# Chunk 3's Q, K and V as one run of paired half-height products, chunk 4's moved into the second gate-up stage, and the first down stage's pieces at given tiles

## The chip, the cores and the metric

The kernel runs on one core of one Trainium2 chip. The metric is device time in microseconds (us), the median over runs. The core's engines are TensorE (PE, matrix products; its weight loads are listed as PEld), VectorE (DVE), ScalarE (ACT), GpSimd (POOL) and SyncE (SP). Every engine works through its own instructions in the order in which the program emits them; they meet through semaphores. SP and POOL issue most transfers; these land later, moved by the core's 16 DMA engines.

## The reference

A transformer block with conditioning: a layer norm, modulated by a row vector; attention with 32 heads of 18 columns, in which each position sees 8 positions at distance 2; a residual; a second norm; a gated bilinear feed-forward (the gate has no nonlinearity); a second residual. All in bfloat16, with 2048 positions, D = 576 and F = 4608.

```python
mod = (silu(c) @ w_mod).reshape(1, 6, 1, 576)        # sa, ca, ga, sb, cb, gb
h = layernorm(x) * (1 + ca) + sa
q, k, v = split(h @ wqkv)                            # 32 heads of 18
idx = pos[:, None] - 2 * arange(8)[None, :]          # masked where negative
attn = softmax(q . k[idx] * 18 ** -0.5)
x = x + ga * ((attn . v[idx]) @ wo)
h = layernorm(x) * (1 + cb) + sb
x = x + gb * (((h @ w_gate) * (h @ w_up)) @ w_down)
```

## The kernel before

**Tiling.** Positions are cut into 8 chunks of 256 (two row tiles of 128) for the attention part, and into 5 groups of row tiles for the feed-forward (`GROUPS`, L43): tiles 0-1, 2-5, 6-9, 10-12 and 13-15. Group 1 is chunks 1 and 2. For each group there is a gate-up stage (`gate_up`, L758) and then a down stage (`down`, L814). What the attention part of later chunks needs is put as small pieces among the products of these stages: an attention piece is a Python function that emits its instructions when it is called, so the order of calls is the order of work on every engine.

**Down stage.** For each of the 36 steps `f` (128 rows of the hidden dimension each) and each row tile `j` of the group, `mm_a` multiplies by 512 columns of the down weights and `mm_r` by the remaining 64; the sums stay in PSUM banks (8 in all; the first down stage keeps 3). The last four steps run tile by tile, so that the evictions of one tile run beside the products of the next. Down weights come in blocks of four steps: when block b is done, block b + 3 is asked for on POOL's queue, into the buffer that became free (3 buffers). `spread` (L748) sets the pieces at equal distances over the steps.

**Pieces of chunk i, by name.** `a_ln`: statistics of the first norm (DVE). `a_norm`: reciprocal deviation (ACT, two instructions), normalization (DVE). `a_t`: ten transposes (PE), then five modulated column blocks into `hT`, by default three on DVE and two on ACT. `a_q` (5 groups) and `a_v` (2 row tiles): Q, K and V by plain products with 128 rows of contraction; the 576 rows are 4.5 times 128, and the fifth product's lower half is zero. `b_mul`, `b_add`: attention times values, summed (DVE); the last writes `o_sb`. `b_o`: output transposes (PE), three copies into `oT` (ACT). `b_w(i, j)`: output projection of a row tile (PE), gate and residual (DVE), giving `x1`. `b_ln`, `b_norm`: second norm. `b_t`: transposes (PE) and the modulated columns into `h2T` (three DVE, two ACT): the operand of the group's gate-up stage. In the first down stage, `gb_row` makes the feed-forward's gate row, chunk 1 and chunk 2 go through `b_o` to `b_t`, chunk 3 and chunk 4 through `a_ln` to `a_v`, and `av2` holds the fourteen value pieces of chunk 2.

**Pairs of half-height products.** A product with 64 rows of contraction uses half the array, and two of them, on the upper and the lower rows (`LO`, `HI`, L526), run side by side. `pair_unit` (L542) takes two results at once: in `first`, one is built from the upper 64 rows of the five row blocks and the other from the lower ones; in `second`, after a wait for the last product of its own `first` (`swap_after`), the halves change places. Nine half steps then do what five whole ones did, if the odd 64 rows of the contraction lie in both halves: `load_pair_rows` (L535) copies the last 64 rows of the Q, K and V weights into the lower half (SP transfers, a POOL copy into `wq4`, and two ACT copies of the modulation). `qkv_units` (L565) makes five such units of a chunk: Q, K, the fifth tile of Q and K, and two of V. In `gate_up` units stand between the steps: the `first` of the next item goes ahead of the `second` of the one before. `PAIRED` (L42) names the chunks whose Q, K and V are made like this: 5 in the second gate-up (its last steps), 6 in the third (its first steps), 7 in the fourth.

**Queues around it.** `ahead` (L803) emits the loads of later gate-up weights on SP; `gb_row` (L1157) emits POOL's loads of down weight blocks 1 and 2 and of chunk 2's values.

Of the kernel before, what the change touches and what calls it, by code (L numbers as in the profile page):

```python
# [28 lines left out]
FT = FF // P  # L29
# [6 lines left out]
FB = 4  # L36
# [2 lines left out]

MODK = (0, 4, 1, 2, 3)  # L40
QKK = (0, 1, 4, 2, 3)
PAIRED = (5, 6, 7)  # L42
GROUPS = [(0, 2), (2, 6), (6, 10), (10, 13), (13, 16)]  # L43


# [1 line left out]
def kernel(  # L47
# [133 lines left out]
    def behind(dma, load):  # L181
        tc.add_manual_dep(dma.ins, load.ins.name, SYNC, reason="value rows go first")
# [168 lines left out]
    def a_norm(i):  # L351
        aa[i]["rsq"]()
        aa[i]["norm"]()
# [181 lines left out]
    def load_pair_rows():  # L535
        nc.sync.dma_start(wqk[64:, KF, :], A_wqkv[KF * P:D, 0:2 * D])
        nc.sync.dma_start(wv[64:, KF, :], A_wqkv[KF * P:D, 2 * D:3 * D])
        nc.gpsimd.tensor_copy(halves(wq4[64:, KF, :]), halves(wqk[64:, KF, :])[:, :, KF * P:D])
        for r in (LO, HI):
            nc.scalar.copy(modc[r, 0:2, KT], modc[0:64, 0:2, KF])  # L540
# [24 lines left out]
    def qkv_units(i, plan):  # L565
        qT, kT = qTs[i % 2], kTs[i % 2]
        vs = []

        def qk_op(m, cols=slice(0, CH)):
            return lambda k: (qk_w(k, m), aa[i]["hT"][:, k, cols])  # L570

        def v_op(j, hf):
            return lambda k: (aa[i]["hT"][:, k, js(j)], wv[:, k, 288 * hf:288 * (hf + 1)])

        def q_out(a, b):
            nc.scalar.copy(qT[:, 0:2, :], a[:])
            nc.scalar.copy(qT[:, 2:4, :], b[:])

        def k_out(a, b):
            nc.scalar.copy(kT[:, 0:2, HALO:], a[:])  # L580
            nc.scalar.copy(kT[:, 2:4, HALO:], b[:])

        def qk4_out(a, b):
            for j, t in enumerate((a, b)):
                nc.scalar.copy(kT[0:64, KF, HALO + j * P:HALO + (j + 1) * P], t[64:P, 0, :])
                nc.scalar.copy(qT[:, KF, js(j)], t[:, 0, :])
            a_halo(i)

        def v_out(hf):
            def out_(a, b):  # L590
                for j, t in enumerate((a, b)):
                    if hf == 0:
                        vs.append(vstage.tile([P, DH, H], BF, name="v_sb"))
                    nc.scalar.copy(vs[j][:, :, 16 * hf:16 * (hf + 1)], t[:, 0, :].rearrange("p (h d) -> p d h", d=DH))
                    if hf == 1:
                        r0 = HALO + i * CH + j * P
                        nc.gpsimd.dma_start(vd[r0:r0 + P, :], vs[j][:].rearrange("p d h -> p (d h)"))
            return out_

        units = ([pair_unit(CH, [(qk_op(m), qk_op(m + 2)) for m in (0, 1)], q_out),  # L600
                 pair_unit(CH, [(qk_op(m), qk_op(m + 2)) for m in (KT, KT + 1)], k_out),
                 pair_unit(P, [(qk_op(KF, js(0)), qk_op(KF, js(1)))], qk4_out)]
                + [pair_unit(288, [(v_op(0, hf), v_op(1, hf))], v_out(hf)) for hf in range(2)])
        return {f: units[a:b] for f, a, b in plan}

    keyed = []

# [195 lines left out]
    def ahead(gi, n):  # L803
        g = gi * NBLK + n + 2
        if gi > 0:
            load_wgu(g)
        elif n in (1, 2, 3):
            load_wgu(g + 2)
        elif n == 4:
            load_wgu(NBLK - 1)  # L810
        elif n in (6, 7, 8):
            load_wgu(n + 3)

    def down(gi, hh, bg):  # L814
        t0, t1 = GROUPS[gi]
        nj = t1 - t0
        final = gi == NG - 1
        last = FT - (2 if final else 1) * FB
        at = spread([(1.0, p) for p in bg], last)
        acc = [ps([P, 512], F32, "acc") for _ in range(nj - final)]  # L820
        halves = [(ps([P, CH], F32, "acc"), slice(CH * h, CH * (h + 1))) for h in range(2)] if final else []
        accr = ps([P, 2 * ST, 64], F32, "accr")

        def mm_a(f, j):
            wb = wd_blk[gi * NBLK + f // FB]
            for a, cs in [(acc[j], slice(0, 512))] if j < len(acc) else halves:
                nc.tensor.matmul(a[:], lhsT=hh[:, f, js(j)], rhs=wb[:, f % FB, cs], start=(f == 0), stop=(f == FT - 1))  # L827

        def mm_r(f, j):
            wb = wd_blk[gi * NBLK + f // FB]  # L830
            nc.tensor.matmul(accr[:, j, :], lhsT=hh[:, f, js(j)], rhs=wb[:, f % FB, 512:D],  # L831
                             start=(f == 0 and j == 0), stop=(f == FT - 1), skip_group_check=True)

        for f in range(last):
            for j in range(nj):
                mm_a(f, j)
                mm_r(f, j)
            if f % FB == FB - 1:
                load_wd(gi * NBLK + f // FB + 3)
            for piece in at[f]:  # L840
                piece()
        xs = [x1[t // ST][t % ST] for t in range(t0, t1)]
        if final:
            for j in range(nj):
                for f in range(last, FT - FB):
                    mm_r(f, j)
            for j in range(len(acc)):
                for f in range(last, FT - FB):
                    mm_a(f, j)
        for j in range(nj):  # L850
            for f in range(FT - FB, FT):
                mm_r(f, j)
        o_ts = [gup.tile([P, 512], BF, name="o_t", tag="g_sb" if j % 2 else "u_sb") for j in range(nj)]
        t_r = smp.tile([P, 2 * ST, 64], BF, name="t_r", tag="tree")
        nc.vector.tensor_tensor(t_r[:, 0:nj, :], accr[:, 0:nj, :],
                                gb_bc[:, None, 512:D].to_broadcast([P, nj, 64]), ALU.mult)
        if final:
            for j in range(nj):
                nc.vector.tensor_tensor(xs[j][:, 512:D], t_r[:, j, :], xs[j][:, 512:D], ALU.add)
            for j in range(nj):  # L860
                r0 = (t0 + j) * P
                for a, cs in [(acc[j], slice(0, 512))] if j < nj - 1 else halves:
                    for f in range(FT - FB if j < len(acc) else last, FT):
                        wb = wd_blk[gi * NBLK + f // FB]
                        nc.tensor.matmul(a[:], lhsT=hh[:, f, js(j)], rhs=wb[:, f % FB, cs], start=False, stop=(f == FT - 1))
                    nc.vector.tensor_tensor(o_ts[j][:, cs], a[:], gb_bc[:, cs], ALU.mult)
                    nc.vector.tensor_tensor(xs[j][:, cs], o_ts[j][:, cs], xs[j][:, cs], ALU.add)
                    stored = slice(0, CH) if cs.stop == CH else slice(cs.start, D)
                    nc.sync.dma_start(out_flat[r0:r0 + P, stored], xs[j][:, stored])
            return  # L870
        for j in range(nj):
            for f in range(last, FT):
                mm_a(f, j)
            nc.vector.tensor_tensor(o_ts[j][:], acc[j][:], gb_bc[:, 0:512], ALU.mult)
        for j in range(nj):
            r0 = (t0 + j) * P
            nc.vector.tensor_tensor(xs[j][:, 0:512], o_ts[j][:], xs[j][:, 0:512], ALU.add)
            nc.vector.tensor_tensor(xs[j][:, 512:D], t_r[:, j, :], xs[j][:, 512:D], ALU.add)
            nc.sync.dma_start(out_flat[r0:r0 + P, :], xs[j][:])
        load_wd(gi * NBLK + NBLK + 2)  # L880
# [264 lines left out]
           3: B_one(7, [(0.0, lambda: b_ld(7, 0)), (0.0, lambda: behind(b_ld(7, 1), wgu_in[3 * NBLK + 4]))], B_av(7)) + [res(7)],  # L1145
           4: [(1.0, nop), (1.0, early_wd)]}
    av2 = [p for _, p in B_av(2)]
    oq = out_qkv(1, 3)
    first = []
    while oq or av2:  # L1150
        if oq:
            first.append(oq.pop(0))
        if len(first) > 3:
            first += [p for p in av2[:2]]
            del av2[:2]

    def gb_row():  # L1157
        mod_row(lambda p, k: wm5[p, k, :] if k < KF else wm5r[p, :], gb_bc, sc_bc2)()
        behind(load_wd(1), wgu_in[4])
        behind(b_ld(2, 0), wgu_in[7])  # L1160
        load_wd(2)
        b_ld(2, 1)

    dbg = {0: [gb_row] + first + out_qkv(2, 4) + [load_pair_rows],
           1: out_qkv(3, 5) + out_qkv(4, 6),
           2: out_qkv(5, 7) + out_qkv(6, 8),
           3: [nop, lambda: b_t(6, (1,))] + out_qkv(7, 8)}
    units = {1: qkv_units(5, [(29, 0, 1), (30, 1, 2), (31, 2, 3), (32, 3, 4), (33, 4, 5)]),
             2: qkv_units(6, [(0, 0, 1), (1, 1, 2), (2, 2, 3), (3, 3, 4), (4, 4, 5)]),
             3: qkv_units(7, [(0, 0, 3), (1, 3, 4), (2, 4, 5)])}  # L1170
    for gi in range(NG):
# [3 lines left out]
            hhp = pool("hhp", 1)  # L1175
        hh = hhp.tile([P, FT, 2 * CH], BF, name="hh") if gi else hh0
        gate_up(gi, hh, gbg.get(gi, []), units.get(gi, {}), 2 if gi == 3 else 0)
        down(gi, hh, dbg.get(gi, []))


# [28 lines left out]
```

## Time and profile before

| | us |
|---|---|
| median of 3 runs | 555.68 |
| lowest, highest | 555.51, 556.32 |
| the profiled execution | 556.14 |
| its span | 554.4 |

The granted clock was 1.00 throughout. The profile is of the one profiled execution, and its times count from the start of the span. By the order of time, the first gate-up ends and the first down stage starts with a product at 88.96; the second gate-up's first product is at 132.59, the second down stage's at about 213.4, the third gate-up's at 256.66.

A row of the page's groups gives instructions of one line, engine, tile and shape: how many, their summed busy time, and the mean duration of one. Matmuls overlap, so their durations (0.38 us for 512 columns) are longer than the distance from one start to the next (0.21 us), and PE's cost is read from starts. A row of a table by stretch has the length, then busy time and count of PE, PEld, DVE, ACT and POOL, then the granted clock, DMA share and GB/s. In an order of time each row has start, duration (of the merged run), engine, line, operation, result and operands, shapes and count, and in brackets the idle time before it with what ended it.

| first down stage, 88.96 to 132.59 | start to start, us |
|---|---|
| one step of two row tiles (0.22 + 0.03, twice) | 0.49 |
| gb row, 89.46 to 90.68 | 1.22 |
| output transposes, 91.17 to 91.73 | 0.56 |
| projection of a row tile, 96.90 to 98.12 | 1.22 |
| chunk 3's transposes, 94.86 to 96.14 (waits in it) | 1.28 |
| value product of a row tile, 109.93 to 111.15 | 1.22 |

### The profile page before, as it was taken

To read this page: it belongs to the slowest core of one execution; us is meant where nothing else is said; L and a number is where in the kernel's file an instruction comes from. 1 tells how busy PE (TensorE), PEld (TensorE's weight loads), DVE (VectorE), ACT (ScalarE), POOL (GpSimd) and SP (SyncE) were. 2 spreads that over 40 slices of the span, in tenths; PEclk is the share of its full clock that TensorE was granted. 3 is DMA by queue.
4 is the path that set the end of the run, shared out by engine and by line. 5 is a ranking of instruction groups with operands and counts; after the bars stand their busy time and mean duration, and the time that the engine had idled before them with its cause. 6 is when DMAs were issued, how large, how long until landed. Compare 5 with 4: busy or idle time off the path is not lost.

```text
span 554.4 us, 14594 instructions
## 1 busy us (share of the span) xinstructions
PE 544.1 (98%) x6160; PEld 323.9 (58%) x6195; DVE 330.5 (60%) x796; ACT 251.8 (45%) x592; POOL 63.7 (11%) x98
## 2 busy tenths in 40 slices
PE   7999999999999999999999999999999999999997
PEld 4888886665444465555544445556656555555564
DVE  7888898985669763557267786444627615322202
ACT  2746666344565664212656553113566511455500
POOL 3102201123000001112000100111100022200010
PEclk9999999999999999999999999999999999999999
DMA  8999999746646844336624775435595665976031
GB/s 267 273 286 321 348 316 329 221 145 195 228 150 195 272 147 141 97 122 196 244 80 151 238 224 176 128 100 160 189 289 173 196 189 182 319 224 186 2 86 32
DMA packets 70155, 108.38 MB, mean 195 GB/s; under 512 B 3690, under 2 KB 57850, under 8 KB 70090
## 3 DMA queue, kind: packets, MB, share of 16 engines
q1 hardware_dynamic: 58832, 61.50, 36.6%
q0 software_dynamic: 11168, 45.81, 25.9%
q8 instruction: 48, 0.79, 0.6%
q10 hardware_dynamic: 90, 0.15, 0.1%
q14 instruction: 17, 0.14, 0.1%
HBM read 103.00 MB, written 4.44 MB: 194 GB/s over the span
## 4 chain that ended last, share of the span: by engine, by line
PE 84%; DMA 9%; DVE 6%; ACT 1%; issue 1%; SPq 0%
PE pg L529 28%; PE pu L529 22%; PE acc L827 19%; PE pp L529 4%; PE accr L831 3%; DMA wgr<-in_B_w_gate_dram 3%; PE pw L674 2%; DMA wo<-in_A_wo_dram 2%; PE lg L448 2%; DMA wgu<-in_B_w_gate_dram 1%; DMA x_t<-in_A_x_dram 1%; DVE vsh L501 1%; PE pq L385 1%; DVE ln_xn L272 1%; DMA wmA<-in_w_mod_dram 1%
## 5 line engine op out<-in xcount | busy, mean ns | idle before, releaser
L529 PE MATMUL pg<-h2T,wgu 64*128 64x512 bf16 (+2 forms) x1440 | 279.1, 333 | 0.0
L529 PE MATMUL pu<-h2T,wgu 64*128 64x512 bf16 (+2 forms) x1440 | 278.3, 333 | 0.0
L529 PEld LDWEIGHTS <-wgu 64*128 64x128 bf16 x2880 | 140.4, 94 | 105.0
L785 ACT CAST u_sb<-pu 128x512 bf16<-128x512 f32 (+2 forms) x180 | 90.1, 500 | 130.6 <-PE pg L529 128.7
L827 PE MATMUL acc<-wd,hh 128*128 128x512 bf16 (+1 forms) x522 | 131.0, 372 | 0.2
L791 DVE TENSOR_TENSOR hh<-g_sb,u_sb 128x512 bf16<-128x512 bf16 (+2 forms) x180 | 66.1, 369 | 106.3 <-ACT g_sb L786 104.3
L831 PE MATMUL accr<-wd,hh 128*128 128x64 bf16 x528 | 93.7, 193 | 1.2
L786 ACT CAST g_sb<-pg 128x512 bf16<-128x512 f32 (+2 forms) x180 | 91.4, 508 | 0.0
L827 PEld LDWEIGHTS <-hh 128*128 128x128 bf16 x588 | 55.3, 98 | 59.5 <-issue 1.7
L529 PE MATMUL pg<-h2T,wgr 64*128 64x512 bf16 (+2 forms) x180 | 60.2, 334 | 0.2 <-DMA wgu<-in_B_w_gate_dram 0.2
L529 PE MATMUL pu<-h2T,wgr 64*128 64x512 bf16 (+2 forms) x180 | 60.2, 334 | 0.0
L166 POOL DMA_DIRECT2D wd<-in_B_w_down_dram x41 | 30.8, 751 | 237.1 <-PE accr L831 213.5
L831 PEld LDWEIGHTS <-hh 128*128 128x128 bf16 x576 | 51.7, 98 | 1.7
L501 DVE TENSOR_TENSOR vsh<-vsh,attn 128x1152 bf16<-128x1152 bf16 x56 | 40.4, 750 | 0.0
L438 DVE TENSOR_TENSOR prod<-qT,kT 128x1280 bf16<-128x1280 bf16 x46 | 37.1, 828 | 4.3 <-ACT kT L364 4.3
L529 PEld LDWEIGHTS <-wgr 64*128 64x128 bf16 x360 | 17.6, 94 | 16.3 <-issue 3.6
L427 POOL DMA_DIRECT2D vsh<-vd x14 | 12.5, 894 | 118.2 <-DVE o_sb L512 83.1
L676 DVE TENSOR_TENSOR x<-pw,ga_bc 128x512 bf16<-128x512 f32 x14 | 9.6, 687 | 25.7 <-PE pw L674 25.7
L294 DVE TENSOR_SCALAR h2T<-tr_pA,modc 128x256 bf16<-128x256 bf16 (+1 forms) x27 | 8.8, 382 | 26.2 <-PE tr_pA L307 26.2
L267 ACT ACTIVATE ln_rstdb<-ln_mvb,eps 128x2 f32<-128x2 f32 (+1 forms) x9 | 2.7, 296 | 44.6 <-DVE ln_mvb L264 44.6
L296 ACT ACTIVATE h2T<-tr_pB,modc 128x256 bf16<-128x256 bf16 (+1 forms) x16 | 7.7, 533 | 30.5 <-PE tr_pB L307 30.5
L508 DVE TENSOR_TENSOR vsh<-vsh 128x1152 bf16<-128x1152 bf16 x28 | 20.5, 750 | 0.0
(219 smaller groups left out, 553.4 us busy)
## 6 DMA issues: line engine op xcount, KB each, us to landing
wd<-in_B_w_down_dram POOLq DMA_DIRECT2D x41, 576.0 KB, 4.4
wgu<-in_B_w_gate_dram SPq DMA_DIRECT2D x45, 512.0 KB, 4.2
wgu<-in_B_w_up_dram SPq DMA_DIRECT2D x45, 512.0 KB, 5.7
vsh<-vd POOLq DMA_DIRECT2D x14, 1152.0 KB, 8.5
x_r<-in_A_x_dram SPq DMA_DIRECT2D x8, 288.0 KB, 7.3
vsh<-in_B_w_down_dram POOLq DMA_DIRECT2D x4, 576.0 KB, 9.4
out_dram<-x SPq DMA_DIRECT2D x15, 144.0 KB, 4.3
x_t<-in_A_x_dram SPq DMA_DIRECT2D x7, 288.0 KB, 6.7
```

The lines of the kernel that those rows point to most:

```text
L166: return nc.gpsimd.dma_start(wb[:], B_w_down[r0:r0 + FB * P, :].rearrange("(k p) n -> p k n", p=P))
L427: return nc.gpsimd.dma_start(vsh[:].rearrange("p w d h -> p w (d h)"), vsrc)
L438: nc.vector.tensor_tensor(prod[:], aa[i]["qT"][:], aa[i]["kT"][:, :, off:off + CH], ALU.mult)
L448: nc.tensor.matmul(b["lg"][H * wl:H * (wl + 1), wq, :], lhsT=ind[:, m, :], rhs=b["prod"][4 * wq + wl][:, m, :], start=(m == 0), stop=(m == ...
L501: nc.vector.tensor_tensor(v, v, at, ALU.mult)
L508: nc.vector.tensor_tensor(vsh[:, d], vsh[:, d], vsh[:, 4 + 2 * s:6 + 2 * s], ALU.add)
L529: return nc.tensor.matmul(dst, lhsT=lhs, rhs=rhs, start=first, stop=last, skip_group_check=True)
L785: nc.scalar.copy(u[:, 0:N], pu[:, 0:N])
L786: nc.scalar.copy(g[:, 0:N], pg[:, 0:N])
L791: nc.vector.tensor_tensor(hh[:, f, 0:N], g[:, 0:N], u[:, 0:N], ALU.mult)
L827: nc.tensor.matmul(a[:], lhsT=hh[:, f, js(j)], rhs=wb[:, f % FB, cs], start=(f == 0), stop=(f == FT - 1))
L831: nc.tensor.matmul(accr[:, j, :], lhsT=hh[:, f, js(j)], rhs=wb[:, f % FB, 512:D], start=(f == 0 and j == 0), stop=(f == FT - 1), skip_grou ...
```

## The change

Chunks 3 and 4 join the paired ones. Chunk 3's five units are run as one block (`qkv_block`) after step 11 of the first down stage: V's two units, the deviation of chunk 1's second norm, Q and K, then the fifth tile; inside each of the three, the `first` of all units goes before the `second` of all. Chunk 4's units go into the second gate-up's first five steps. The pieces of the first down stage are no longer spread evenly but stand at steps given by hand (several in other orders than before: the first value pieces of chunk 2 ahead of chunk 3's normalization); its two `a_t` leave one column block to DVE and four to ACT. Chunk 2's second norm is done by row tile, `b_t` of its first tile after step 31, and of its second one between the last products of the two row tiles. The pair rows are loaded during the first gate-up, and put in place within `gb_row`.

```diff
-PAIRED = (5, 6, 7)
+PAIRED = (3, 4, 5, 6, 7)
...
     def load_pair_rows():
         nc.sync.dma_start(wqk[64:, KF, :], A_wqkv[KF * P:D, 0:2 * D])
         nc.sync.dma_start(wv[64:, KF, :], A_wqkv[KF * P:D, 2 * D:3 * D])
+
+    def place_pair_rows():
         nc.gpsimd.tensor_copy(halves(wq4[64:, KF, :]), halves(wqk[64:, KF, :])[:, :, KF * P:D])
         for r in (LO, HI):
             nc.scalar.copy(modc[r, 0:2, KT], modc[0:64, 0:2, KF])
...
+    def qkv_block(i, between):
+        q, k, qk4, v0_, v1_ = qkv_units(i, [(0, 0, 5)])[0]
+        for pair in ((v0_, v1_), (q, k), (qk4,)):
+            for part in range(2):
+                for unit in pair:
+                    unit[part]()
+            if pair[0] is v0_:
+                between()
...
         elif n == 4:
             load_wgu(NBLK - 1)
+        elif n == 5:
+            load_pair_rows()
         elif n in (6, 7, 8):
             load_wgu(n + 3)
-    def down(gi, hh, bg):
+    def down(gi, hh, bg, late=nop):
...
-        at = spread([(1.0, p) for p in bg], last)
+        at = bg if gi == 0 else spread([(1.0, p) for p in bg], last)
...
         for j in range(nj):
             for f in range(last, FT):
                 mm_a(f, j)
+            if j == 0:
+                late()
             nc.vector.tensor_tensor(o_ts[j][:], acc[j][:], gb_bc[:, 0:512], ALU.mult)
...
-    oq = out_qkv(1, 3)
-    first = []
-    while oq or av2:
-        if oq:
-            first.append(oq.pop(0))
-        if len(first) > 3:
-            first += [p for p in av2[:2]]
-            del av2[:2]
-
     def gb_row():
         mod_row(lambda p, k: wm5[p, k, :] if k < KF else wm5r[p, :], gb_bc, sc_bc2)()
         behind(load_wd(1), wgu_in[4])
         behind(b_ld(2, 0), wgu_in[7])
+        place_pair_rows()
         load_wd(2)
         b_ld(2, 1)
 
-    dbg = {0: [gb_row] + first + out_qkv(2, 4) + [load_pair_rows],
+    ln2 = []
+
+    def last_ln(j):
+        if j == 0:
+            ln2.extend(ln_parts(lambda j: x1[2][j], "b"))
+            bb[2]["xn"] = ln2[0]
+        else:
+            x_res.pop(2)
+        ln2[1](j)
+        ln2[2](slice(j, j + 1))
+
+    def last_norm(j):
+        ln2[3](j)
+
+    def av(n):
+        for p in av2[:n]:
+            p()
+        del av2[:n]
+
+    at0 = [[] for _ in range(FT - FB)]
+    for f, piece in ((0, gb_row), (0, lambda: a_ln(3)), (1, lambda: b_o(1)), (2, lambda: av(2)), (3, lambda: (a_norm(3), load_x(5))),
+                     (4, lambda: b_w(1, 0)), (5, lambda: av(2)), (6, lambda: a_t(3, (0,))), (7, lambda: b_w(1, 1)), (8, lambda: av(2)),
+                     (9, lambda: b_ln(1)), (10, lambda: av(1)), (11, lambda: qkv_block(3, bb[1]["rsq"])), (11, lambda: bb[1]["norm"]()), (12, lambda: av(4)),
+                     (13, lambda: b_t(1)), (15, lambda: av(3)), (19, lambda: a_ln(4)), (22, lambda: b_o(2)), (23, lambda: (a_norm(4), load_x(6))),
+                     (25, lambda: b_w(2, 0)), (25, lambda: last_ln(0)), (26, lambda: b_w(2, 1)), (26, lambda: last_ln(1)), (27, lambda: a_t(4, (0,))),
+                     (30, lambda: last_norm(0)), (30, lambda: last_norm(1)), (31, lambda: b_t(2, (0,)))):
+        at0[f].append(piece)
+
+    dbg = {0: at0,
            1: out_qkv(3, 5) + out_qkv(4, 6),
...
-    units = {1: qkv_units(5, [(29, 0, 1), (30, 1, 2), (31, 2, 3), (32, 3, 4), (33, 4, 5)]),
+    units = {1: qkv_units(4, [(0, 0, 1), (1, 1, 2), (2, 2, 3), (3, 3, 4), (4, 4, 5)]) | qkv_units(5, [(29, 0, 1), (30, 1, 2), (31, 2, 3), (32, 3, 4), (33, 4, 5)]),
...
-        down(gi, hh, dbg.get(gi, []))
+        down(gi, hh, dbg.get(gi, []), (lambda: b_t(2, (1,))) if gi == 0 else nop)
```

## The prediction

> **What bounds the kernel now.** I read the page first: busy shares and the chain that ended last.
>
> ```profile
> PE 544.1 (98%) x6160; PEld 323.9 (58%) x6195; DVE 330.5 (60%) x796; ACT 251.8 (45%) x592; POOL 63.7 (11%) x98
> ...
> PE 84%; DMA 9%; DVE 6%; ACT 1%; issue 1%; SPq 0%
> ```
>
> TensorE (PE) sets the time over the whole, so a change is worth what it takes off PE, unless PE then waits. Next, busy time by stretch: the first down stage (88.96 to 132.59 us, from its first product to the next stage's first) and the third gate-up, which already opens with paired Q, K and V as the second one will.
>
> ```profile
> 88.96:132.59 43.63, 42.62 (x381) 26.95 (x386) 35.15 (x91) 19.76 (x52) 10.14 (x15) 1.00 0.63 193
> ...
> 256.66:336.00 79.34, 79.34 (x859) 39.15 (x860) 55.21 (x112) 44.51 (x88) 5.42 (x7) 1.00 0.60 193
> ```
>
> VectorE (DVE; behind the length come PE, weight loads, DVE) is busy 35.15 of the down stage's 43.63 us: it has not much less to do than PE. The chain of waits, in order of time, says so too:
>
> ```profile
> 106.13 2.07 DVE vsh L501 x3
> 108.20 1.10 DVE ln_xn L272 x4
> ...
> 117.45 0.61 DVE x L676
> 118.10 1.24 PE pw L674 x5
> ```
>
> Up to 118 us this stage's chain runs through DVE; only behind that, where Q, K, V of chunk 4 lie, through PE. DVE's own order of time shows that it is through early and then waits for PE:
>
> ```profile
> 123.35 1.18 DVE L272 TENSOR_SCALAR ln_xn<-x,ln_mvb,ln_rstdb 128x576 bf16<-128x576 bf16 x4 [0.60 <-ACT ln_rstdb L268]
> 127.19 1.05 DVE L294 TENSOR_SCALAR h2T<-tr_pA,modc 128x256 bf16<-128x256 bf16 x3 [2.65 <-PE tr_pA L307]
> 130.96 0.29 DVE L855 TENSOR_TENSOR t_r<-accr,gb_bc 128x128 bf16<-128x128 f32 x1 [2.73 <-PE accr L831]
> ```
>
> So PE work that leaves this stage's end is gained only until DVE's chain, ending at 124.5 us, becomes the end.
>
> **The change, part by part.** Prices are start-to-start distances on PE.
>
> ```profile
> 100.08 1.26 PE L385 MATMUL pq<-hT,wqk 128*128 128x256 bf16 x10
> 101.18 0.38 PE L827 MATMUL acc<-wd,hh 128*128 128x512 bf16 x1
> 101.39 0.19 PE L831 MATMUL accr<-wd,hh 128*128 128x64 bf16 x1
> 101.42 0.38 PE L827 MATMUL acc<-wd,hh 128*128 128x512 bf16 x1
> ```
>
> ```profile
> 260.78 2.13 PE L529 MATMUL pp<-hT,wqk 64*128 64x256 bf16 x36
> 262.75 0.38 PE L529 MATMUL pu<-h2T,wgu 64*128 64x512 bf16 x1
> ```
>
> *Q, K, V of a chunk.* Plain: ten products 1.09 us, so 4.5 such groups 4.91; V twice 1.22 (109.93 to 111.15): 7.35. Paired, in the third gate-up: 1.09 + 1.97 + 1.15 + 0.83 + 1.11 + 0.49 (each from the unit's start to the next gate-up product) = 6.64. Two chunks: 1.4 us less PE work, and one chunk's 6.64 moves into the second gate-up. There I charge it in full: the third gate-up carries the same units in the same five places and has 79.34 busy of 79.34.
>
> *What remains in the down stage.* One of its 36 steps (two row tiles) takes 0.49. I followed PE, DVE and ScalarE (ACT) piece by piece, each in its order, with rows' durations; the same count over the old order puts the next stage's first product at 132.47, where the trace has 132.59.
>
> Steps 0 to 11: 5.89 and the gb row 1.22, output transposes 0.56, projections 2 x 1.22, chunk 3's transposes 0.56, which wait 0.78 for DVE's normalization (two value products now stand before it): 88.96 to 100.4. The block: V 2.20, then 0.17 until V's first bank is evicted, Q and K 3.92, the fifth Q/K tile 0.28 + 0.22 with a wait of 0.20 between (its second half waits for its own first half, and step 12 is queued behind), and a change to 64 rows and back, 2 x 0.10 as at the stage's start (88.75 to 88.96 where a product takes 0.11): 107.6. Steps 12 to 22 with chunk 1's transposes: 113.5.
>
> The Trainium skill, TensorEngine Tiling (Array Packing), Key Properties, says that changing the tiling mode drains TensorE, which speaks against a paired block among full-height products. As an estimate from it, each change would cost the rest of a 0.27 us product, 0.16, and the stage would be 0.12 longer; the row of 0.10 decides.
>
> *The new end.* Chunk 2's output transposes end at 114.1. Behind them, one after the other: ACT's three oT copies to 115.6, the reciprocal deviation of chunk 4 (queued behind these copies) to 116.1, DVE's normalization 1.32, x of tile 4 1.22, its statistics 0.95, x of tile 5 1.22, statistics 0.95, one hT column block 0.32, normalization of tile 4 0.64: 122.7. PE has its 32 steps done at 121.5 and waits 1.28. Then transposes 0.28, 64-column remainder 0.23, four steps 0.86, transposes 0.28, four steps 0.86, switch 0.10: 125.4. ACT is later: the last deviation ends at 122.4, behind it four hT blocks (4 x 0.455) and four halves of h2T (4 x 0.345): 125.6. The second gate-up starts at 125.66, 6.81 before the 132.47 of the same count.
>
> **Sum:** -6.81 + 6.64 = -0.17 us: the 1.4 us of pairing and some 2 us of old waits come back as new waits (0.78 + 0.17 + 0.20 + 1.28 + 0.28 = 2.71). The profiled execution took 556.14 with a span of 554.4; less 0.2 it is 555.9, and the median of 555.68 becomes 555.5.
>
> *Moved at no cost.* The two transfers of the pair rows (0.22 MB) go on SP's queue from 126.8 and 130.7 us to behind weight block 8 (issued 69.5 to 72.2) and before block 9 (77.4): cover is the idle quarter of the DMA at 76 to 80 us (share 0.77 and 0.72); without it they delay by 0.6 us (0.22 MB at 350 GB/s) blocks that the second gate-up needs 30 us later. POOL's copy of 0.29 moves from 132.16 to between the issues at 79.68 and 91.11, into 10.55 us of POOL idling. ACT's two copies (0.40) move from 131.15 to 91.44, before the oT copies of 91.82; oT is then late by some 0.02, and its reader stands two steps later than before. Chunk 3's value rows leave at 104 instead of 112 us, chunk 4's some 11 us later than now, both long before they are read. Two modulations less per chunk on DVE (4 x 0.32) are four more on ACT (0.455 each): counted above.
>
> *Bounds where no row shows the thing.* Waits of PE in the new stage: none at best, 2.7 less; bank of Q: at worst it waits for V's last eviction, 0.9 more instead of 0.17 (I take the oldest bank first). Second gate-up: at best its own waits near 185 us (0.9) vanish, at worst its evictions queue (about 1). Down weights: below.
>
> **Rivals.**
> 1. *The tiles hide the waits* (faster). If statistics, normalizations and evictions fall into PE's 32 steps, PE never waits: -0.17 - 2.71, so 552.8; half of it, 554.2. For it: DVE's total shrinks by 1.3 us, and its old waits for ACT (0.60 three times) could close. Against: tile 4's and 5's x, statistics and normalization stand behind chunk 2's projection, PE's own late product.
> 2. *Down weights come late* (slower). Block 6 of the down weights is asked for when step 15 frees its buffer, 110.1, and used at step 24, 114.6: 4.5 us, since steps 14 to 22 now run bare. Landings in this stage took from 4.4 us (late in it) to 7.1. Lateness up to 0.35 hides behind DVE's normalization of chunk 4; from a landing of 4.85 on it shifts the end one for one: at 5.4, 556.0; at 7.1, 2.25 more, 557.8. For it: six of the nine landings issued from 91 to 130 us took over 4.85. Against: five of these six were issued before 108 us, with DMA shares of 0.5 to 1.0; from 112 to 122 us, with less traffic as there would be here, they took 4.4 to 4.7.
> 3. *The moved units don't fit* (slower). The second gate-up has chunk 5's units and transposes too; ACT is busy 46.5 of 80.8 us there. If evictions of chunk 4 hold banks, a wait of 0.2 at each of five units: 556.5. Against: the third gate-up.
>
> **How the numbers follow.** A measurement of this kernel tells about 0.2%, 1.1 us, from no change. Forecast 50% (its own range 554.6 to 556.4), rival 1 25%, rival 2 15%, rival 3 10%. Faster: four fifths of rival 1 and a fifth of the forecast's, 0.30. Slower: two thirds of rivals 2 and 3 and some of the forecast, 0.23. The rest, 0.47, within. Range 553.2 to 557.2: below lies only rival 1 in full, above only the latest landing.
>
> **What would show it.** After: the first gate-up product of the second group at 125.7 (123 for rival 1, over 127 for rival 2); a PE wait near 121.5 released by DVE's normalization, ACT as the last releaser; step 24's wait, if any, released by a DMA of the down weights; paired products of 2.2 + 3.9 + 0.7 us in one run; the second gate-up 87.4 long. It is wrong if DVE ends before PE's step 31, if a bank or weight wait over 0.5 us stands in the block or at step 24, or if the second gate-up grows by other than 6.6.

## The result, and the profile after

| | before | after |
|---|---|---|
| median of 22 runs, us | 555.58 | 556.76 |
| lowest, highest | 554.88, 557.02 | 555.90, 558.17 |
| the profiled execution, its span | 556.14, 554.4 | 556.8, 555.1 |
| first down stage, first product to the next stage's first | 43.63 | 38.23 |
| second gate-up, likewise | 80.85 | 87.49 |

The changed kernel takes 1.002 of the time before (95% interval 1.0014 to 1.0026): 1.2 us slower. The two stages say the same: -5.40 + 6.64 = +1.24. The second down stage has its 43.22 us in both. So the place to look is the first down stage, which was to become 6.81 us shorter.

First the changed kernel's page: busy time, share of the span and instructions of each engine; and the shares of the chain of waits.

```profile
PE 543.2 (98%) x6283; PEld 326.2 (59%) x6317; DVE 329.5 (59%) x795; ACT 254.5 (46%) x604; POOL 65.8 (12%) x98
...
PE 83%; DMA 9%; DVE 3%; issue 2%; ACT 1%; POOL 0%; SPq 0%; POOLq 0%
```

PE has 0.9 us less work, and the program is 1.2 us longer. The table by stretch (length, then PE, weight loads, DVE, ACT, POOL; granted clock, DMA share, GB/s) shows where PE stands still:

```profile
88.37:126.60 38.23, 34.81 (x376) 21.88 (x381) 34.07 (x91) 17.60 (x51) 8.95 (x13) 1.00 0.74 235
126.60:214.09 87.49, 87.44 (x999) 47.20 (x998) 58.94 (x123) 51.30 (x106) 6.38 (x9) 1.00 0.55 179
```

In the down stage 3.42 us without work on PE, where it was 1.01 before; in the second gate-up 0.05. The chunk that moved there is paid at full price, as forecast, and nothing more. PE's order of time names the places, each with the idle time and what ended it in brackets:

```profile
100.48 2.38 PE L529 MATMUL pp<-wv,hT 64*128 64x288 bf16 x36 [0.92 <-ACT hT L296]
...
107.62 0.39 PE L840 MATMUL acc<-wd,hh 128*128 128x512 bf16 x1
...
115.82 0.38 PE L840 MATMUL acc<-wd,hh 128*128 128x512 bf16 x1 [1.03 <-DMA wd<-in_B_w_down_dram]
...
123.44 0.34 PE L307 MATMUL tr_pA<-ident,ln_xn 128*128 128x128 bf16 x3 [0.53 <-DVE ln_xn L272]
...
126.60 0.37 PE L529 MATMUL pg<-h2T,wgr 64*128 64x512 bf16 x1 [0.47 <-ACT h2T L296]
```

Four waits, 2.95 us together: at the block's start for ACT's column blocks, at step 24 for down weights, for the second norm of tile 4, and for ACT's last columns. The block itself is well sized (100.48 to 107.62, 7.14; forecast 7.19). The first two waits are new; the chain of waits (start, us, what) leads through both to the late end:

```profile
98.96 1.47 ACT hT L296 x3
...
100.48 1.91 PE pp L529 x28
...
110.61 5.17 DMA wd<-in_B_w_down_dram
...
115.82 0.38 PE acc L840
...
116.96 1.09 PE pw L685 x5
...
118.08 0.18 DVE x L687
```

Two steps on, behind steps 24 and 25, comes the output projection of tile 4 (116.80 in PE's order, 116.96 in the chain), and everything of the stage's end, x, statistics, normalization, columns, is queued behind that product on DVE and ACT. A wait of PE at step 24 therefore moves the end, though PE waits for DVE anyway later.

DVE's order of time, two rows, answers to the ones shown of before:

```profile
118.08 0.69 DVE L687 TENSOR_TENSOR x<-pw,ga_bc 128x512 bf16<-128x512 f32 x1 [0.86 <-PE pw L685]
...
122.96 1.31 DVE L272 TENSOR_SCALAR ln_xn<-x,ln_mvb,ln_rstdb 128x576 bf16<-128x576 bf16 x4
```

DVE waits 0.86 for PE's late projection: in my count it had no such gap. Its last normalization is no longer preceded by a wait for ACT (0.60 before).

### The profile page after: what moved, and what is told of

The parts are those of the page before. It is cut to its first block, busy times and chain, and to the rows that moved or that the text cites. A ratio compares the mean times of both kernels' runs of the same rounds, so it can differ in the third digit from the quotient of the medians.

```text
span 555.1 us, 14848 instructions
## 1 busy us (share of the span) xinstructions
PE 543.2 (98%) x6283; PEld 326.2 (59%) x6317; DVE 329.5 (59%) x795; ACT 254.5 (46%) x604; POOL 65.8 (12%) x98
## 4 chain that ended last, share of the span: by engine, by line
PE 83%; DMA 9%; DVE 3%; issue 2%; ACT 1%; POOL 0%; SPq 0%; POOLq 0%
PE pg L529 28%; PE pu L529 22%; PE acc L840 19%; PE pp L529 5%; PE accr L844 3%; DMA wgr<-in_B_w_gate_dram 3%; PE pw L685 2%; DMA wo<-in_A_wo_dram 2%; PE lg L448 2%; DMA wgu<-in_B_w_gate_dram 1%; DMA x_t<-in_A_x_dram 1%; DMA wd<-in_B_w_down_dram 1%; DMA wmA<-in_w_mod_dram 1%; ACT hT L296 1%; PE tr_pA L307 0%
## 5 line engine op out<-in xcount | busy, mean ns | idle before, releaser
L294 DVE TENSOR_SCALAR h2T<-tr_pA,modc 128x128 bf16<-128x128 bf16 (+1 forms) x30 | 9.5, 371 | 24.7 <-PE tr_pA L307 24.7
L529 PE MATMUL pp<-hT,wqk 64*128 64x256 bf16 x360 | 22.0, 269 | 0.0
```

The lines of the kernel that those rows point to most:

```text
L529: return nc.tensor.matmul(dst, lhsT=lhs, rhs=rhs, start=first, stop=last, skip_group_check=True)
```

## The experiments

The two candidates for the lost time are the two new waits. All kernels compute the whole reference. Ratios are to the kernel before, whose median beside them was 555.92 (the first four) and 555.91 (the last three).

| kernel | median, us | ratio (95% interval) | first down stage, us |
|---|---|---|---|
| weights' buffer | 555.92 | 1.0005 (0.9994 to 1.0016) | 37.10 |
| column block by PSUM tile | 556.44 | 1.0016 (1.0005 to 1.0027) | 37.35 |
| both | 554.99 | 0.9985 (0.9972 to 0.9998) | 36.30 |
| plain block | 555.37 | 0.9996 (0.9985 to 1.0006) | 36.96 |
| plain block with both | 555.19 | 0.9987 (0.9977 to 0.9996) | 36.16 |
| other order | 553.83 | 0.9960 (0.9947 to 0.9972) | 34.92 |
| only chunk 4's move | 561.31 | 1.0092 (1.0077 to 1.0108) | 44.30 |

The second gate-up took 87.48 or 87.49 us in every one, so the stage's length tells them apart. The lengths come from one profiled execution of each kernel, the times from 5 to 12 runs of it. Read from PE's order of time, the stage falls into parts:

| kernel | stage starts | block starts, into the stage | block takes | step 12 to the next stage |
|---|---|---|---|---|
| changed kernel | 88.37 | 12.11 | 7.14 | 18.98 |
| weights' buffer | 88.60 | 11.93 | 7.14 | 18.03 |
| column block by PSUM tile | 88.64 | 11.13 | 7.14 | 19.08 |
| both | 88.57 | 11.13 | 7.14 | 18.03 |
| plain block | 88.42 | 11.03 | 7.62 | 18.31 |
| plain block with both | 88.21 | 10.77 | 7.36 | 18.03 |

**A buffer of its own for weight block 6.** It can then be asked for before step 15 frees one: at 104.86 instead of 110.61.

```diff
-        wb = wdp.tile([P, FB, D], BF, name="wd")
+        wb = wgx.tile([P, FB, D], BF, name="wgu") if g == 6 else wdp.tile([P, FB, D], BF, name="wd")
```

> The changed kernel, with block 6 of the down weights in a buffer that is free since the first gate-up, so that POOL can ask for it as soon as chunk 3's value rows are written (about 105 us) instead of after step 15 (110.6). Theory (late weights cost what DVE's slack does not absorb): the 1.03 us wait at step 24 is gone, the wait for tile 4's normalization behind step 31 grows from 0.5 to 1.0, and the first down stage shortens from 38.23 to 37.74, 0.49 less. Rival (the end of the stage is DVE's and ACT's alone): the wait goes, the stage stays 38.2.

Measured: 37.10, so 1.13 us less, more than the expected 0.49: 0.95 behind the block and 0.18 ahead of it. PE's order of time:

```profile
100.53 2.38 PE L529 MATMUL pp<-wv,hT 64*128 64x288 bf16 x36 [0.45 <-ACT hT L296]
...
122.53 0.34 PE L307 MATMUL tr_pA<-ident,ln_xn 128*128 128x128 bf16 x3 [0.77 <-DVE ln_xn L272]
...
125.70 0.37 PE L529 MATMUL pg<-h2T,wgr 64*128 64x512 bf16 x1 [0.38 <-ACT h2T L296]
```

The wait of 1.03 at step 24 is gone, and 0.95 has come off the end; the wait for tile 4's normalization grew only from 0.53 to 0.77. (The 0.18 is not the buffer's doing, which is first used at 104.86: the block starts when ACT's columns are there, at the same time in both, 100.48 and 100.53, and this stage began 0.23 later. PE waits only 0.45 there because it has already waited 0.32 for weights at step 8.) I had left DVE some slack to swallow part of the lateness; it has none, since its normalization of chunk 4 takes 1.19, not the 1.32 that I counted, and it was the one that waited. The rival, by which the stage would have stayed at 38.2, falls.

**One column block by PSUM tile.** Transposes of a chunk go into two PSUM tiles, `tr_pA` (column blocks 0 to 2) and `tr_pB` (3 and 4). The change leaves block 0 to DVE and the rest to ACT, so both read `tr_pA`. Here DVE has block 3 in its place, and ACT has a whole `tr_pA`.

```diff
-(6, lambda: a_t(3, (0,)))
+(6, lambda: a_t(3, (3,)))
```

> The changed kernel, with column block 3 instead of block 0 of chunk 3's modulation left to DVE, so that ACT starts with blocks 0 to 2 of the PSUM tile that DVE does not read; counts per engine are the same. Theory (ACT waited because DVE had the first block of the same PSUM tile, and DVE was late with it): ACT starts right behind the transposes, about 95.9 instead of 98.50, the 0.92 us wait of PE ahead of the paired block goes, and the first down stage shortens by 0.92 to 37.3. Rival (the tail decides and earlier waits are absorbed): the wait goes, the stage stays within 0.3 of 38.2.

Measured: 37.35, 0.88 us less: the block starts 0.98 earlier, and step 24 waits 0.10 longer, for a landing of 5.27. By the medians alone this edit isn't clear of noise (a ratio of 1.0016 against 1.0020). ACT's order of time, first in the changed kernel, then here:

```profile
98.50 1.02 ACT L296 ACTIVATE hT<-tr_pA,modc 128x256 bf16<-128x256 bf16 x2 [4.74 <-DVE hT L294]
99.41 1.02 ACT L296 ACTIVATE hT<-tr_pB,modc 128x256 bf16<-128x256 bf16 x2
```

```profile
96.09 1.48 ACT L296 ACTIVATE hT<-tr_pA,modc 128x256 bf16<-128x256 bf16 x3 [2.05 <-PE tr_pA L307]
98.78 0.56 ACT L296 ACTIVATE hT<-tr_pB,modc 128x256 bf16<-128x256 bf16 x1 [1.21 <-DVE hT L294]
```

In the changed kernel all four ACT blocks, those of `tr_pB` too, stand behind one DVE block of 0.41 us that began at 98.06. Given its own tile, ACT starts 2.4 us sooner, when PE's transposes end, and only the block that shares a tile with DVE's still waits for DVE. The paired block then starts without a wait. In the kernel before the split was by tile, which is why its ACT had nothing of DVE to wait for (ACT's order of time, then DVE's):

```profile
96.12 1.02 ACT L296 ACTIVATE hT<-tr_pB,modc 128x256 bf16<-128x256 bf16 x2 [1.78 <-PE tr_pB L307]
```

```profile
98.25 1.04 DVE L294 TENSOR_SCALAR hT<-tr_pA,modc 128x256 bf16<-128x256 bf16 x3
```

These two rows also answer a rival, that ACT waits because both write `hT`: in program order DVE's three blocks stand ahead there too, and ACT wrote its own 2 us before them.

The Trainium skill, PSUM — Partial Sum Buffer, section on bank collisions, says that two engines must not touch one PSUM bank in the same partitions at the same time, reads against reads included, and that a program has to guard PSUM by semaphores, by bank and quadrant of partitions or, more simply, by bank. The trace agrees with such an order: 98.50 against 96.09 for the same ACT work. What happens without it was not tried.

**Both.**

> Both edits of the two runs above. Theory: the two waits add up to what the forecast missed: the first down stage 36.8 long (38.23 less 0.92 less 0.49), the time 1.4 under the changed kernel, that is 555.4, within 0.2 of the kernel before. Rival (something else in the change costs the time, such as the earlier load of the pair rows or the longer second gate-up): it stays at 556.3 or above.

Measured: 36.30. The two gains add up: 0.98 at the block's start and 0.95 behind the block are the 1.93 found. The program is now a little faster than before the change (the interval ends at 0.9998), and its median is 0.93 under the first experiment's. What is left of waits on PE are 0.77 for DVE's last normalization and 0.38 for ACT's last columns, as in the first experiment's rows: the two forecast waits of the new end, at 1.15 instead of 1.28 + 0.28.

**Chunk 3 by plain products**, in the same place; chunk 4 stays paired. This prices the pairing within the block.

```diff
-PAIRED = (3, 4, 5, 6, 7)
+PAIRED = (4, 5, 6, 7)
...
+    def plain_block(i, between):
+        a_v(i, 0)
+        a_v(i, 1)
+        between()
+        for g in range(5):
+            a_q(i, g)
...
-(11, lambda: qkv_block(3, bb[1]["rsq"]))
+(11, lambda: plain_block(3, bb[1]["rsq"]))
```

> The changed kernel, with chunk 3's block as plain products in the same place (V of both row tiles, then Q, the fifth tile, K); chunk 4 stays paired. Theory (in a block of its own the pairing gives up most of its gain to the wait for the bank, the wait for its own first half and the two mode changes): the block takes 7.35 instead of 7.14, and the stage is 0.1 to 0.2 longer. Rival (pairing is worth 0.7 here as it is between the gate-up steps): the stage is 0.6 to 0.7 longer, the time above 557.3.

Measured: 36.96, 1.27 us shorter than with pairs, where both theories expected it longer. PE's order of time:

```profile
99.45 1.48 PE L408 MATMUL pv<-wv,hT 128*128 128x504 bf16 x5
...
114.59 0.38 PE L847 MATMUL acc<-wd,hh 128*128 128x512 bf16 x1 [0.36 <-DMA wd<-in_B_w_down_dram]
```

There is no wait at the block's start. A plain run begins with column block 0, which DVE delivers first; a run of pairs begins with the fifth one, the odd 64 rows, which ACT delivers last. Inside the plain run PE still waits for columns: its first five products take 1.48 (1.23 in the next experiment), and the block 7.62 instead of the expected 7.35. Even so step 12 comes at 18.65 us into the stage instead of 19.25: 0.60. The rest is the weights: asked for 4.18 us before they are needed in both (110.61 to 114.79, 110.05 to 114.23), they landed in 4.50 here and in 5.17 in the changed kernel: 0.67. Why they landed sooner here stays open; the DMA moved 274 GB/s from 112 to 114 us here and 247 there, and with DVE's block 3 (second experiment) the landing took 5.27 at 274.

**The plain block with both cures**, so that neither wait blurs the price of pairing.

> Both fixes (weights early, column block 3 to DVE), with chunk 3's block as plain products in the same place. Theory (plain was ahead in the earlier run because its first products need the first column blocks, which ACT delivers first, while a pair starts with the last one; without that wait the paired block is ahead by 0.2): the stage is 36.5, against 36.30 with pairs. Rival (a block of plain products is quicker as such): 35.8 or less.

Measured: 36.16, against 36.30 with pairs. The block took 7.36 (98.98 to 106.34) by plain products and 7.14 by pairs, so pairing saves 0.22 inside it, where I had counted 7.35 against 7.19. That the stage is shorter all the same comes from ahead of the block, where the two kernels do the same work: PE's transposes waited 0.26 less in this profile, of the quickest of twelve runs (second tile 6.81 us into the stage, with pairs 7.07). From these transposes to the next stage it is 29.35 (95.02 to 124.37) by plain products and 29.23 (95.64 to 124.87) by pairs: the pairs save 0.22 in the block and lose 0.10 at its start, 4.06 instead of 3.96 behind the transposes, as much as the forecast counted for one change to 64 rows. So for chunk 3 pairing is worth about 0.1 us, too little to show in the medians (554.99 and 555.19).

**Another order of the pieces.** Kept from the change: what is paired, and the weights' buffers. Moved: the column block (to block 3 in both `a_t`), and from step 13 on chunk 4's statistics and normalization and chunk 2's outputs and projections go two to four steps earlier, with the fourth `av` ahead of them and `a_t` of chunk 4 between the projections.

```diff
-(6, lambda: a_t(3, (0,)))
+(6, lambda: a_t(3, (3,)))
...
-                      (13, lambda: b_t(1)), (15, lambda: av(3)), (19, lambda: a_ln(4)), (22, lambda: b_o(2)), (23, lambda: (a_norm(4), load_x(6))),
-                      (25, lambda: b_w(2, 0)), (25, lambda: last_ln(0)), (26, lambda: b_w(2, 1)), (26, lambda: last_ln(1)), (27, lambda: a_t(4, (0,))),
-                      (30, lambda: last_norm(0)), (30, lambda: last_norm(1)), (31, lambda: b_t(2, (0,)))):
+                      (13, lambda: av(3)), (14, lambda: b_t(1)), (16, lambda: a_ln(4)), (18, lambda: b_o(2)), (19, lambda: (a_norm(4), load_x(6))),
+                      (21, lambda: b_w(2, 0)), (23, lambda: a_t(4, (3,))), (23, lambda: last_ln(0)), (24, lambda: b_w(2, 1)), (24, lambda: last_ln(1)),
+                      (28, lambda: last_norm(0)), (28, lambda: last_norm(1)), (31, lambda: b_t(2, (0,)))):
```

> The changed kernel with other steps for the pieces behind the block: chunk 2's last value pieces at step 13 and chunk 1's transposes at 14, statistics of chunk 4 at 16, output transposes of chunk 2 at 18, normalization of chunk 4 at 19, projections of tiles 4 and 5 at 21 and 24 with their statistics, chunk 4's transposes at 23, the last normalizations at 28; column block 3 to DVE. The weights keep their buffers. Theory (what is left after the two fixes is DVE's chain, lengthened by its own idle time at 109 and 116 us, and bare steps in front of the weights): both go, step 24 comes over 6 us after step 15, PE waits for no normalization behind step 31, the first down stage is 35.3 long (36.3 with both fixes), the time 1.7 us under the kernel before. Rival (DVE's amount of work sets the stage, not its order): 36.3 or more.

Measured: 34.92, and 553.83 us, 2.1 us under the kernel before and the fastest of all. The table by stretch for this stage, and its end in PE's order of time:

```profile
88.54:123.46 34.92, 34.73 (x383) 21.83 (x382) 33.29 (x90) 18.35 (x51) 8.80 (x12) 1.00 0.74 236
```

```profile
120.74 0.33 PE L307 MATMUL tr_pA<-ident,ln_xn 128*128 128x128 bf16 x3
...
123.46 0.37 PE L529 MATMUL pg<-h2T,wgr 64*128 64x512 bf16 x1
```

PE is busy for all but 0.19 us, and no row of the stage has a bracket. DVE has 33.29 us of work in a stage of 34.92 and does not hold PE up: the waits came from the order of the pieces, not from DVE's amount of work, as the rival had it. A projection and chunk 4's transposes now stand ahead of step 24, so it is reached later, 5.79 us behind the request (109.80 to 115.59), and its weights come in time without a buffer of their own.

**Only chunk 4's move**: the old code, spread evenly, with chunk 4's units taken to the second gate-up and chunk 3 plain.

```diff
-PAIRED = (5, 6, 7)
+PAIRED = (4, 5, 6, 7)
```

(with `units` as in the change, and the pair rows loaded early and put in place in `gb_row`, as there).

> The kernel before, with one part of the change: chunk 4's Q, K and V as pairs in the second gate-up's first five steps (and the pair rows loaded early); chunk 3 plain and all pieces spread evenly as before. Theory (the products of chunk 4 were the cover of DVE's last chain): PE waits some 2.7 us for chunk 2's last normalization, the first down stage is 39.1 long instead of 43.63, 4.5 less for 6.64 more in the gate-up, so 2.1 us slower than before. Rival (DVE keeps up): the stage is 7.4 shorter, 0.7 us faster than before.

Measured: 44.30, in an execution of 563.53, the slowest of five (the others took 560.40 to 562.31; if the rest took the same there, their stage was some 1 to 3 us shorter, an estimate). It has the wait for chunk 2's last normalization that was expected (2.41 against 2.7), and one that was not. PE's order of time, a row of the chain of waits, and the table by stretch:

```profile
104.42 0.38 PE L831 MATMUL acc<-wd,hh 128*128 128x512 bf16 x1 [4.08 <-DMA wd<-in_B_w_down_dram]
...
104.91 1.90 PE L385 MATMUL pq<-hT,wqk 128*128 128x256 bf16 x10
...
109.63 1.26 PE L385 MATMUL pq<-hT,wqk 128*128 128x256 bf16 x10
...
130.41 0.34 PE L307 MATMUL tr_pA<-ident,ln_xn 128*128 128x128 bf16 x3 [2.41 <-DVE ln_xn L272]
```

```profile
93.21 11.17 DMA wd<-in_B_w_down_dram
```

```profile
102.00:104.00 2.00, 0.00 (x0) 0.00 (x0) 1.97 (x6) 0.00 (x0) 0.00 (x0) 1.00 0.99 332
104.00:106.00 2.00, 1.58 (x12) 1.11 (x12) 1.93 (x7) 0.00 (x0) 0.00 (x0) 0.84 0.42 150
106.00:108.00 2.00, 2.00 (x10) 0.99 (x9) 2.00 (x5) 0.98 (x3) 0.00 (x0) 0.50 0.05 16
108.00:110.00 2.00, 2.00 (x16) 1.14 (x15) 2.00 (x7) 0.00 (x0) 0.40 (x1) 0.81 0.00 0
```

Step 12 comes 7.1 us after its weights were asked for, as in the kernel before (94.70 to 101.87), but there they landed in 7.1 and here in 11.2, with the DMA full (share 0.99). PE waits 4.08 us, and behind the wait the granted clock is 0.84, 0.50 and 0.81 for three slices, with ten Q/K products at 1.90 us instead of 1.26. The Trainium skill, TensorE: Matmul & The Clock Gate, The HAM clock gate, gives half rate behind an idle window of about 3.4 us; the 0.50 behind 4.08 us agrees. Less this wait, the stage would have 40.2 us, and less the clock's loss, an estimate of 1.3 to 1.7 us from the three slices, 38.5 to 38.9: near the 39.1 expected. The landing is long in the changed kernel too: 10.1 us, asked for at 92.58. There chunk 3's block stands ahead of step 12, so that the weights are not needed before 107.62. Two things differ from the kernel before in both: the pair rows are loaded ahead of the stage, and two weight blocks are asked for within 2.05 us instead of 3.59. Which of them makes the landing long was not tried. So this kernel shows that the old order doesn't bear the move together with the early load; what the move would cost by itself stays open.

## Why the prediction missed

The forecast was 555.5 and no measurable difference; the measured time is 1.2 us above the kernel before. Of the 1.53 us by which the new stage is longer than forecast, 0.67 stand at the block's start and some 0.9 behind the block. Point by point:

- **The moved chunk** (+6.64): measured 87.49 - 80.85 = 6.64. Right, and rival 3 (units that don't fit) falls: PE waits nowhere inside this stage.
- **The block** (7.19): measured 7.14. Right as a whole.
- **Rows of the old stage**: 43.51 counted, 43.63 in the trace. So the whole miss is in the new one: 36.70 forecast, 38.23 measured, +1.53.
- **The failing step** is "Two modulations less per chunk on DVE (4 x 0.32) are four more on ACT (0.455 each): counted above". The work was counted, but not the wait: I let ACT start its four blocks when PE's transposes were done, and did not see that DVE's one block shares `tr_pA` with two of them. The block starts 12.11 us into the stage instead of 11.44. I had forecast a wait of 0.78 at the transposes in its place; their second tile starts 0.55 behind the first, where 0.28 is work, so that wait was smaller and this one came on top. With the split by tile the block starts 11.13 us into the stage, and the stage is 0.88 shorter.
- **Mis-sized in rival 2**: "Lateness up to 0.35 hides behind DVE's normalization of chunk 4; from a landing of 4.85 on it shifts the end". The place, the releaser and the mechanism were as described. Landing 5.17 in 4.18 us, not 4.5: the lead was 0.3 smaller than counted and the landing 0.3 above the turning point. And the cover was not there: 0.13 of the 0.35 was the 1.32 for a normalization that takes 1.19, and DVE waited for PE, not PE for DVE. The rival's price for a landing of 5.17 was 0.32; taking the wait away gave 0.95. At 15% I held it too unlikely: the quickest landing of a down block in the whole changed kernel took 4.2 us, and the median one 4.6, so a lead of 4.18 left next to none that would have come in time. In the forecast's own sum this wait stood at nothing.
- **The new end**: forecast waits 1.28 and 0.28; measured 0.53 and 0.47 in the changed kernel, 0.77 and 0.38 once the two other waits are gone. Right in place and releasers (DVE's normalization, then ACT), too large in the first.
- **"Moved at no cost"** was right for PE in the changed kernel, which waits for no weights before step 24. But the landings behind the early pair rows grew: weight block 3 took 10.1 us there instead of 7.1, outside the 4.4 to 7.1 that the forecast had reckoned with, and PE waited for weights at step 8 of the first experiment (0.32) and at step 12 of the last. Whether the pair rows or the closer requests did it was not tried.
- **Rival 1** (no waits, 552.8) is what the new order comes near to: 553.83, and a stage of 34.92 with no wait, where the rival's would have been 33.99. The condition for it that I gave, that the evictions and norms fall into PE's steps, was met by the order of pieces, not by the change as it stood.
- **Pairing**: "the 1.4 us of pairing" is not there for chunk 3: its pairs save 0.22 in the block, give back 0.10 at its start, and in the changed kernel more than the rest by starting on the last column block. Chunk 4's share was not measured apart from its move.

The text had named the sign of its failure, a bank or weight wait over 0.5 us in the block or at step 24: 1.03 at step 24, and 0.92 at the block's start, behind the shared PSUM tile.

## What to carry to other kernels

Work taken off a busy engine also takes away the cover it gave to the transfers and to the other engines: before moving it, count for each buffer how much work stands between its release and its next use, and compare that with the slowest landing that the trace shows, not the usual one. And count it with the new transfers in place: the landings of before need not hold after the move (7.1 became 10.1 here). When evictions are shared between two engines, see that the one with more of them doesn't stand behind the other's block in a shared PSUM tile, and begin the products with the column blocks that come first, where the kernel leaves the choice. If waits appear although no engine is full, try the order of the pieces: here it was worth, with the split by tile, 3.3 us of the stage (38.23 to 34.92), more than the pairing.

## What the runs showed of the hardware

- The same 576 KB block of down weights landed in 4.50, 5.17 and 5.27 us in three kernels, at a similar place, with the DMA idle when it was asked for (share 0.00 from 108 to 110 us in all three).
- Down weights asked for some 4 to 6 us into the stage landed in 7.1 us in the kernel before and in 8.5 to 11.2 in the eight others, with DMA shares of 0.89 to 1.12 from 92 to 104 us in the changed kernel (0.64 to 1.03 before).
- DVE's four normalizing instructions took 1.18 or 1.19 us as a rule, and 1.31 to 1.41 in several cases in which POOL issues a weight block inside them (the changed kernel: 1.31 from 122.96 with an issue at 123.21). Not in every one: in the first experiment both started at 122.06, and it was 1.18. This is a coincidence seen in rows, not a cause that was tried.
